# An already tuned three-stage fp32 kernel on one core: the second MLP's input product done as Strassen's seven half-size products, with streamed weights and one written instruction list

## The chip, the core and the metric

The kernel runs on one NeuronCore of a Trainium2 chip. Its engines run side by side, each through its own instruction list and in that list's order: TensorE (PE) multiplies matrices, VectorE (DVE), ScalarE (ACT) and GpSimd (POOL) work elementwise, and SyncE (SP) issues the transfers between DRAM and the on-chip memory SBUF. TensorE writes only to PSUM, eight banks of 128 partitions by 512 fp32 columns; ACT and DVE read the results from there. The metric is the device time of one execution in microseconds (us); lower is better.

## The reference

Three stages follow each other on 2304 tokens (T): a decayed linear attention of 4 batches, 8 heads, 576 positions; a first MLP (512 to 1024 to 512 with softmax, gating and layer norm); a second MLP (512 to 2048 to 512):

```python
h = x @ w_in                     # x: 2304 x 512, w_in: 512 x 2048
g = np.where(h >= 1, h, np.where(h <= -1, 0.0, (h + 1) ** 2 / 4.0))
return (g @ w_out).astype(np.float32)
```

Every matmul is in fp32 accuracy: an operand is split into a rounded part (hi) and the rest (lo), and a product is three TensorE matmuls, hi*lo, lo*hi and hi*hi, summed in PSUM. The weights arrive as 64-bit words and are first turned into fp32 on the chip.

## The kernel before

**Stages and their lists.** The attention, the first MLP and the preparation of all weights stand in ORDER, a table of words that one loop plays: each word (such as `H.3.0.4`) is a step and appends that step's instructions to the engines' lists. Attention steps are `q`, `k` (loads of a 128-token tile), `S`, `I`, `O`, `U` (matmuls) and others; the first MLP has `H` (hidden product, 12 matmuls 512 columns wide), `T` (transposes) and `J` (output product, 48 matmuls 256 wide, of 256 tokens each); `G`, `B` and `t` take its result to DRAM (`xsd`). `l` to `g` turn one unit of weights into hi and lo, `h` makes the sums that Strassen's scheme wants of the second MLP's output weights (on POOL), `s` stores the prepared weights to DRAM (`wid` input weights, `wod` output weights).

**The second MLP** is written out in code behind ORDER. The tokens are cut in blocks of 512 (four, and one last block of 256); the 2048 hidden units in 8 pairs of 128-unit chunks. A *slot* is one block with one pair: 32 slots of 512 tokens, 8 of 256. For each slot `hidden(s, i)` makes chunk i of the pair: 12 matmuls 512 tokens wide (line 565: four 128-row slices of the inner dimension times three matmuls) into the one PSUM bank `h2`. ACT reads it twice (`r`, line 573; `h`, line 574), DVE makes the activation `g` (lines 575 and 580). `factors(s)` makes the seven left factors of Strassen's scheme for the *output* product (line 588) and splits them into `gh` and `gl` (lines 135, 136). `project(s, part)` is that output product: seven half-size products for each 256 tokens, 3 matmuls 256 wide each (line 613), so 42 matmuls for a slot of 512 tokens; they accumulate in the other seven banks over the 8 pairs of a block, and `project_end` adds the sums up (line 643). TensorE's list takes hidden and project in turn, the projection two slots behind:

```python
for s in range(2, len(slots) + 2):
    for i in range(2):
        if s < len(slots):
            hidden(s, i, ps2, "h2")
            ...
        project(s - 2, i)
```

All 16 chunks of the input weights are loaded once and stay in SBUF (`wi`, 512 KB each). The output weights (1792 KB for a pair, as seven half-size matrices, hi and lo) are streamed: three are in SBUF, and `load_wo` fetches the next when one comes free. The blocks go through the pairs alternately forward and backward, so three pairs are met again without a load. PE's and SP's orders in this stage are as the code is written; the other engines' orders are chosen by the framework's scheduler. At the switch from `ps` to `ps2` the second MLP's PSUM banks take the place of the first MLP's.

Of the kernel before, what the change touches and what calls it, by code (L numbers as in the profile page):

```python
# [11 lines left out]
F32 = mybir.dt.float32  # L12
# [10 lines left out]
T = B * S  # L23
DM = H * D
# [16 lines left out]
b.1 O.2 c.1 f.7 V.3 U.2 P.3 H.0.0.4 k.4 W.2 d.1 b.13 D.2 e.8 X.2 g.7 e.1 l.15 a.13.3 f.8 Y.2 c.13 S.4.6.0 f.1
R.0.0 I.3.5 b.9 d.13 g.8 U.3 q.5 a.9.2 V.4 e.13 O.3 W.3 c.9 l.10 b.15 g.1 U.4 k.6 f.13 P.4 I.4.3 d.9 W.4 D.3 O.4
q.6 a.15.0 g.13 X.3 e.9 S.5.6.5 k.5 b.10 c.15 l.12 Y.3 H.0.1.2 f.9 P.5 V.6 a.10.5 D.4 c.10 d.15 X.4 H.1.1.6
R.0.1 d.10 e.15 l.17 f.15 m.0 e.10 V.5 I.5.3 E.0.0 R.1.1 l.19 g.9 E.0.1 U.5 q.8 M.0.0 O.5 f.10 g.15 M.0.1 W.5
z.0 S.6.0.4 k.8 a.12.2 g.10 Y.4 Q.0.0 x.0 I.6.5 P.6 Q.0.1 U.6 q.7 b.12 m.1 w.0 S.8.0.4 E.1.0 c.12 r.0 O.6 D.5
W.6 V.8 N.0.0 M.1.0 H.2.0.3 k.7 E.1.1 d.12 P.8 N.0.1 x.1 X.5 M.1.1 a.17 Y.5 T.0.0.1 z.1 e.12 b.17 I.7.0 Q.1.1
R.2.0 l.20 V.7 H.3.0.4 D.6 K.0.0 c.17 Q.1.0 L.0.0 d.17 f.12 w.1 X.6 g.12 U.7 r.1 a.19 R.3.0 H.3.1.6 Y.6 N.1.1
W.7 e.17 N.1.0 c.19 l.18 a.20 T.1.1.5 b.19 R.3.1 I.8.1 K.1.1 m.3 c.20 b.20 d.19 L.1.1 T.0.1.2 q.9 O.8 K.0.1
L.0.1 b.18 d.20 H.2.1.5 k.9 D.8 e.20 X.8 l.16 Y.8 T.1.0.2 R.2.1 Z.0 f.17 H.4.1.1 V.9 K.1.0 E.3.0 L.1.0 m.2 E.3.1
M.3.0 E.2.0 g.17 J.0.0.2 x.3 E.2.1 s.17 M.2.0 f.20 x.2 a.18 M.2.1 b.16 z.2 M.3.1 Q.2.1 z.3 c.18 Q.2.0 g.20 Q.3.1  # L50
d.18 w.2 S.9.4.3 s.20 G.0.0 U.9 q.13 P.9 r.2 Q.3.0 H.4.0.5 W.9 B.0.0 N.2.0 w.3 t.0.0 N.2.1 e.18 a.16 e.19 l.28
T.2.0.6 R.4.0 r.3 l.24 O.9.3 R.4.1 h.19.0 N.3.0 S.7.4.2 k.11 D.9 h.19.1 N.3.1 J.0.1.3 q.10 P.7 h.19.2 X.9 f.19.0
Y.9 b.28 m.4 g.19.0 a.24 a.28 c.16 b.24 c.28 c.24 V.11 S.10.2.4 K.2.0 G.0.1 L.2.0 d.16 O.7 B.0.1 H.5.0.6 P.10
k.10 h.19.3 t.0.1 d.28 f.19.1 D.7 X.7 e.16 T.3.1.3 g.19.1 l.23 f.16 T.3.0.2 K.3.1 T.2.1.4 R.5.0 V.10 s.19 I.10.0
E.4.0 L.3.1 Y.7 E.4.1 U.10 q.11 M.4.0 K.3.0 O.10 M.4.1 d.24 W.10 z.4 K.2.1 H.5.1.3 k.12 x.4 L.3.0 Q.4.0 L.2.1
Q.4.1 D.10 b.23 w.4 U.11 X.10 R.5.1 r.4 J.1.0.5 W.11 m.5 g.16 N.4.0 e.28 s.16 E.5.0 e.24 l.22 E.5.1 M.5.0 Y.10
l.29 N.4.1 M.5.1 V.12 f.28 z.5 x.5 Q.5.1 g.28 Q.5.0 U.12 s.28 T.4.0.1 G.1.0 w.5 I.11.2 a.23 r.5 B.1.0 f.24 c.23
S.11.4.0 t.1.0 W.12 d.23 N.5.1 I.13.6 q.12 P.11 N.5.0 J.1.1.3 a.22 g.24 b.29 c.22 s.24 b.22 a.29 d.22 c.29 e.22
e.23 l.31 T.5.1.5 K.4.0 d.29 l.30 T.4.1.0 G.1.1 L.4.0 I.12.4 K.5.1 B.1.1 h.23.0 K.4.1 H.8.0.1 L.5.1 t.1.1 h.23.1
L.4.1 b.31 h.23.2 a.31 e.29 f.23.0 H.6.0.3 R.8.0 h.23.3 l.26 b.30 c.31 g.23.0 f.29 a.30 g.29 f.23.1 T.5.0.5  # L60
# [55 lines left out]
def net(ctx: ExitStack, tc: tile.TileContext, qk_t, kv, w_in1, w_out1, g_ln, w_in2, w_out2, masks, decay, out):  # L116
# [198 lines left out]
    def e(u):  # L315
# [232 lines left out]
    def load_wo(s, spare=False):  # L548
# [3 lines left out]
        if p in wo:  # L552
            return
# [216 lines left out]
```

## Time and profile before

| | us |
|---|---|
| median of 3 runs (703.21 to 704.28) | 703.65 |
| the profiled execution's own time | 704.7 |
| its span, first to last instruction | 702.9 |
| TensorE busy in the span | 673.8 |
| VectorE busy | 483.6 |
| ScalarE busy | 364.6 |
| GpSimd busy | 161.8 |

The profiled execution took 1.8 us more than its span, and is 1.05 us above the median of the runs. "Busy" counts an instruction from its start to its end; TensorE's matmuls overlap in the pipeline, so that a busy TensorE can still do more or less work in the same time. Its rate is read from the distance between starts.

### The profile page before, as it was taken

The page shows a single profiled execution, that of the slowest core. Times are in us where ns is not written, and L with a number is a line of the kernel's source. Part 1 is how long each engine was busy: PE and PEld are TensorE (multiplying, and loading weights), DVE is VectorE, ACT ScalarE, POOL GpSimd, SP SyncE. Part 2 cuts the span into 40 slices and gives each one's busy share as a digit, 9 for nine tenths or more (in the row PEclk, how much of TensorE's full clock was granted, in tenths as well). Part 3 has the DMA queues.
Part 4 walks back from the last instruction along what each step waited for, and adds up shares of the span by engine and source line. Part 5 has one row for each costly group of instructions (what it writes and reads, how often), then busy time and mean ns, then how long its engine had stood idle before and what let it go on. Part 6 is the DMA issues. An engine that isn't in the chain of part 4 may idle for free.

```text
span 702.9 us, 12647 instructions
## 1 busy us (share of the span) xinstructions
PE 673.8 (96%) x5000; PEld 603.4 (86%) x5000; DVE 483.6 (69%) x926; ACT 364.6 (52%) x666; POOL 161.8 (23%) x166
## 2 busy tenths in 40 slices
PE   4699999999999999997999999999999999999996
PEld 3587888888988989886998998898898898899996
DVE  4778687878768887544656676657756567556875
ACT  4769768667847678732423433434433343333442
POOL 4987455556365652000000000000000000000000
PEclk9699999999999999999999999999999999999999
DMA  9975569697897897994445315452245403345292
GB/s 334 402 249 208 179 202 368 227 350 267 261 290 269 317 343 295 392 388 154 155 159 210 120 61 210 142 187 106 92 178 210 165 31 133 131 187 210 79 340 91
DMA packets 35547, 152.76 MB, mean 217 GB/s; under 512 B 3616, under 2 KB 11936, under 8 KB 30240
## 3 DMA queue, kind: packets, MB, share of 16 engines
q1 hardware_dynamic: 35200, 151.54, 59.2%
q8 instruction: 39, 0.64, 0.4%
q10 hardware_dynamic: 288, 0.42, 0.2%
q14 instruction: 20, 0.16, 0.1%
HBM read 114.72 MB, written 37.22 MB: 216 GB/s over the span
## 4 chain that ended last, share of the span: by engine, by line
PE 90%; DMA 7%; issue 1%; DVE 1%; ACT 0%; POOL 0%; SPq 0%; DVEq 0%; POOLq 0%; ACTq 0%
PE h L565 29%; PE bank L400 14%; PE bank L502 13%; PE pa L613 7%; PE pb L613 7%; PE pc L613 7%; PE pd L613 4%; DMA qk<-in_qk_t 4%; PE bank L195 2%; PE bank L225 2%; PE bank L472 2%; PE bank L213 2%; DMA kv<-in_kv 2%; DMA st<-in_w_out 2%; PE bank L236 1%
## 5 line engine op out<-in xcount | busy, mean ns | idle before, releaser
L565 PE MATMUL h<-xs,wi 128*128 128x512 f32 (+1 forms) x960 | 215.7, 374 | 3.9 <-issue 3.9
L565 PEld LDWEIGHTS h<-xs,wi 128*128 128x128 f32 x960 | 164.8, 189 | 33.1 <-issue 4.1
L573 ACT ACTIVATE r<-h 128x512 f32<-128x512 f32 (+1 forms) x80 | 44.4, 555 | 163.2 <-PE h L565 163.0
L575 DVE SCALAR_TENSOR_TENSOR r<-r 128x512 f32<-128x512 f32 (+1 forms) x80 | 50.9, 636 | 112.6 <-ACT r L573 112.6
L135 ACT ACTIVATE gh<-gs 128x1024 fp32r<-128x1024 f32 (+1 forms) x80 | 66.9, 873 | 77.5 <-DVE gs L588 73.3
L502 PE MATMUL bank<-ln,wo 128*128 128x256 f32 x864 | 102.1, 278 | 0.0
L502 PEld LDWEIGHTS bank<-ln,wo 128*128 128x128 f32 x864 | 100.4, 188 | 1.2
L400 PE MATMUL bank<-wi1h,x 128*128 128x512 f32 x288 | 90.6, 396 | 0.0
L136 DVE TENSOR_TENSOR gl<-gs,gh 128x1024 fp32r<-128x1024 f32 (+1 forms) x80 | 77.1, 996 | 13.5 <-ACT gh L135 13.5
L310 POOL TENSOR_TENSOR y<-y,st 128x512 int32<-128x512 int32 x48 | 66.6, 1390 | 53.9 <-DVE y L306 27.6
L613 PE MATMUL pb<-wo,gh 128*128 128x256 f32 x288 | 75.2, 283 | 0.0
L400 PEld LDWEIGHTS bank<-wi1h,x 128*128 128x128 f32 x288 | 54.7, 190 | 11.6
L613 PE MATMUL pc<-wo,gh 128*128 128x256 f32 x288 | 63.5, 283 | 0.0
L613 PE MATMUL pa<-wo,gh 128*128 128x256 f32 x288 | 63.0, 281 | 0.0
L588 DVE TENSOR_TENSOR gs<-gs 128x256 f32<-128x256 f32 (+1 forms) x160 | 60.1, 396 | 3.6
L400 PE MATMUL bank<-wi1l,x 128*128 128x512 f32 x144 | 59.7, 415 | 0.0
L580 DVE TENSOR_TENSOR gs<-h,r 128x512 f32<-128x512 f32 (+1 forms) x80 | 51.0, 638 | 7.7 <-DVE r L575 0.9
L613 PEld LDWEIGHTS pb<-wo,gh 128*128 128x128 f32 x288 | 55.0, 191 | 0.0
L613 PEld LDWEIGHTS pa<-wo,gh 128*128 128x128 f32 x288 | 49.5, 190 | 2.6
L613 PEld LDWEIGHTS pc<-wo,gh 128*128 128x128 f32 x288 | 50.0, 192 | 0.0
L574 ACT COPY h<-h 128x512 f32<-128x512 f32 (+1 forms) x80 | 43.1, 539 | 0.0
L613 PE MATMUL pa<-wo,gl 128*128 128x256 f32 x144 | 40.7, 283 | 0.2 <-DVE gl L136 0.2
(82 smaller groups left out, 1080.8 us busy)
## 6 DMA issues: line engine op xcount, KB each, us to landing
wo<-wod SPq DMA_DIRECT2D x28, 1792.0 KB, 7.3
wod<-wo SPq DMA_DIRECT2D x8, 1792.0 KB, 7.3
st<-in_w_in SPq DMA_DIRECT2D x24, 512.0 KB, 6.7
st<-in_w_out SPq DMA_DIRECT2D x24, 512.0 KB, 5.2
qk<-in_qk_t SPq DMA_DIRECT2D x18, 512.0 KB, 5.5
kv<-in_kv SPq DMA_DIRECT2D x18, 512.0 KB, 5.7
xsd<-x SPq DMA_DIRECT2D x36, 256.0 KB, 5.2
wid<-wi SPq DMA_DIRECT2D x16, 512.0 KB, 4.3
```

The costliest lines, as they stand in the source:

```text
L135: nc.scalar.activation(hi, src, AF.Copy)
L136: eng.tensor_tensor(out=lo, in0=src, in1=hi.bitcast(F32), op=ALU.subtract)
L310: nc.gpsimd.tensor_tensor(out=yd[u].bitcast(I32), in0=yd[u].bitcast(I32), in1=raw_w[u][:, :, 0].bitcast(I32), op=ALU.add)
L400: nc.tensor.matmul(hp, a[:, kk, :], w[:, fs], start=(n == 0), stop=(n == 3 * KD - 1))
L502: nc.tensor.matmul(px[:, mm, :], w[:, ms], a[:, f, :], start=(n == 0), stop=(n == 3 * C1 - 1))
L565: nc.tensor.matmul(hp[:, :n], wi[c][:, w, kk], xs[b][:, a, kk], start=(k == 0), stop=(k == 3 * KD - 1))
L573: nc.scalar.activation(r[:, :n], hp[:, :n], AF.Relu, bias=0.5, scale=0.5)
L574: nc.scalar.copy(h[:, :n], hp[:, :n])
L575: nc.vector.scalar_tensor_tensor(out=r[:, :n], in0=r[:, :n], scalar=1.0, in1=r[:, :n], op0=ALU.min, op1=ALU.mult)
L580: nc.vector.tensor_tensor(out=g, in0=h_, in1=r_, op=ALU.max)
L588: nc.vector.tensor_tensor(out=g[:, o], in0=g[:, x], in1=g[:, y], op=op)
L613: nc.tensor.matmul(po[key][:, half], a[:, x, t], wo[p][0][:, w, y], start=(begin and j == 0), stop=(last and j == 2), skip_group_check=True,)
```

## The change

The input product of the second MLP is rewritten for the 32 slots of 512 tokens. The 512 tokens are cut in halves, the 512 inner rows in halves and the pair's 256 hidden units in halves, and Strassen's scheme makes the product from seven products of half size: each is 2 inner slices times 3 matmuls, 256 tokens wide, so 42 matmuls of 256 columns take the place of 24 of 512. The last 256 tokens (`tp`) are multiplied as before, 24 matmuls of 256 columns for a pair.

What goes with it:
- The input weights of a pair become seven half-size matrices, hi and lo, 1792 KB in place of 1024; `h` makes their sums on POOL for both MLP weights. They no longer fit, so they are streamed like the output weights, three pairs in SBUF (`wi`: 23 loads in all; output weights: 27, four of them `wt`).
- The x of a block is loaded raw (`xr`), its four sums are made (`xc`) and its seven factors are split (`xh` on ACT, `xl` on DVE; for block 0 partly on POOL). `B` and the stores of x's lo are gone.
- The seven products of a slot go through *one* PSUM bank in four groups (`hp.s.0` 12 matmuls, `hp.s.1` 6, `hp.s.2` 12, `hp.s.3` 12). After each group ACT copies the bank out (`ha`) before the next group may write. DVE puts the pieces together (`hA`, `hB`); then follow `hr` and `hq` (Relu and Square on ACT), `hm` and `hg` (min and max on DVE), the factors `hf`, and the split `hh`, `hl`.
- The output product (`pp`) is cut in five chunks of 9, 12, 7, 7 and 7 matmuls that stand between the groups. Its last of the seven products is now the one for bank `d`.
- The last 256 tokens' activations go through DRAM once (`ts`, `tL`) and have their output product (`tj`) at the very end, after the last `pp`.
- ORDER runs to the end of the kernel, and sets the order on all engines; the part for the first two stages is a new order too. No bank is set up anew at the switch.

```diff
-C.6 l.6 q.0 k.0 q.1 l.2 l.5 l.0 l.3 k.1 a.6.0 l.11 C.1 b.6 c.6 l.4 S.0.1.2 l.14 d.6 l.8 C.5 C.0 V.0 e.6 C.3 q.2
+C.6 q.0 C.0 k.0 l.1 k.1 q.1 l.3 l.2 l.6 S.0.0.1 l.0 l.7 C.2 l.10 C.5 V.0 P.0 q.2 C.3 l.11 U.0 l.8 a.1.2 C.1 b.1
...
+ha.11.3 wi.14 hf.10.2 hf.10.3 hh.10.0 hA.11 hp.12.0 hh.10.1 hl.10.0 hr.11.0 pp.9.1 hl.10.1 ha.12.0 hB.11 hp.12.1
...
-        y = ws[units[u][1] // 2]
-        o, x, z = ((4, 1, 0), (1, 3, 1), (5, 3, 4), (6, 2, 5))[n]
-        nc.gpsimd.tensor_tensor(out=y[:, o], in0=y[:, x], in1=y[:, z], op=ALU.subtract)
+        y = ws[u]
+        if units[u][0] == 2:
+            o, x, z, op = ((4, 2, 3, ALU.add), (2, 0, 2, ALU.subtract), (5, 4, 0, ALU.subtract), (6, 1, 5, ALU.subtract))[n]
+        else:
+            o, x, z = ((4, 1, 0), (1, 3, 1), (5, 3, 4), (6, 2, 5))[n]
+            op = ALU.subtract
+        nc.gpsimd.tensor_tensor(out=y[:, o], in0=y[:, x], in1=y[:, z], op=op)
...
-        c, n = 2 * p + i, blocks[b][1]
-        hp = pool.tile([P, BLK], F32, tag=tag, name="h2")
-        k = 0
-        for kk in range(KD):
-            for w, a in ((1, 0), (0, 1), (0, 0)):
-                nc.tensor.matmul(
-                    hp[:, :n], wi[c][:, w, kk], xs[b][:, a, kk], start=(k == 0), stop=(k == 3 * KD - 1)
-                )
-                k += 1
+    GROUPS = (((0, 0), (1, 1)), ((2, 1),), ((3, 0), (4, 1)), ((5, 1), (6, 0)))
+    def hp_(s, n, place=7):
+        b, p = slots[s]
+        if n == 0:
+            hp[s] = bank(place, [P, 2, 2 * P])
+        w = resident["wi"][p][0]
+        for o, half in GROUPS[n]:
+            x = xs[b, o][0]
+            k = 0
+            for kk in range(2):
+                for u, a in ((1, 0), (0, 1), (0, 0)):
+                    nc.tensor.matmul(
+                        hp[s][:, half], w[:, u, SLOT[o], kk * P : (kk + 1) * P], x[:, a, kk],
+                        start=(n in (0, 3) and half == 0 and k == 0), stop=(k == 5), skip_group_check=True,
+                    )
+                    k += 1
+            if s % 8 == 7:
+                ring.append(xs.pop((b, o))[1])
+    def ha(s, n):
+        if n == 0:
+            sn[s] = act1.tile([P, 3, 2 * P], F32, tag=f"x1{s % 2}", name="sn")
+        if n == 2:
+            hc[s] = act1.tile([P, 2, 2, 2 * P], F32, tag=f"e{s % 2}", name="hc")
+        if n == 1:
+            nc.scalar.copy(sn[s][:, 0], hp[s][:, 1])
+        else:
+            nc.scalar.copy(sn[s][:, 1:3] if n == 0 else hc[s][:, (1, 0)[n - 2]], hp[s])
+    def hA(s):
+        nc.vector.tensor_tensor(out=hc[s][:, 1], in0=hc[s][:, 1], in1=sn[s][:, 0:2], op=ALU.add)
+    def hB(s):
+        nc.vector.tensor_tensor(out=hc[s][:, 0, 0], in0=hc[s][:, 0, 0], in1=sn.pop(s)[:, 2], op=ALU.add)
+    def hr_(s, k):
+        hr[s, k] = stage.tile([P, 2, 2 * P], F32, tag="y", name="r", bufs=3)
+        nc.scalar.activation(hr[s, k], hc[s][:, 1 - k], AF.Relu, bias=0.5, scale=0.5)
+    def hm(s, k):
+        nc.vector.tensor_scalar(hr[s, k], hr[s, k], 1.0, None, op0=ALU.min)
+    def hq(s, k):
+        nc.scalar.activation(hr[s, k], hr[s, k], AF.Square)
+    def load_for(kind, s):
+        full = len(resident[kind]) == 3
+        if kind == "wo" and s == len(slots) - 1:
+            home = resident["wi"].pop(slots[s - 2][1])[1]
+        else:
+            home = resident[kind].pop(slots[s - 3][1])[1] if full else homes[kind, s]
+        load14(kind, slots[s][1], home)
+    CHUNKS = (0, 9, 21, 28, 35, 42)
+    def pp(s, c):
+        b, p = slots[s]
+        w = resident["wo"][p][0]
+        for i in range(CHUNKS[c], CHUNKS[c + 1]):
+            product(b, i, s % 8 == 0, s % 8 == 7, ghl[s], w)
```

**TensorE's list in the middle of the second MLP, before.** `h` is the hidden bank, `xs` the tokens, `wi` the input weights; `pa`, `pb`, `pd` are banks of the output product; "waits" names the engine whose work the row needs first, DMAHW is a transfer.

```order
L565 MATMUL h_4359<-xs,wi_3710 128x512 [waits Activation_49]
L565 MATMUL h_4359<-xs,wi_3710 128x512 x11
L613 MATMUL pa<-wo_4171,gh 128x256 [waits DMAHW6_49]
L613 MATMUL pa<-wo_4171,gl 128x256 [waits DVE_49]
L613 MATMUL pa<-wo_4171,gh 128x256 x2
L613 MATMUL pa<-wo_4171,gl 128x256
L613 MATMUL pa<-wo_4171,gh 128x256
L613 MATMUL pb<-wo_4171,gh 128x256
L613 MATMUL pb<-wo_4171,gl 128x256
L613 MATMUL pb<-wo_4171,gh 128x256
```

The same place in the changed kernel (the groups `hp` are line 712 with the bank as `bank<-xs,wi`, the chunks `pp` line 799):

```order
L712 MATMUL bank<-xs,wi 128x256 [waits Activation_49]
L712 MATMUL bank<-xs,wi 128x256 x5
L799 MATMUL bank<-wo,gl 128x256
L799 MATMUL bank<-wo,gh 128x256 x2
L799 MATMUL bank<-wo,gl 128x256
L799 MATMUL bank<-wo,gh 128x256 x2
L799 MATMUL bank<-wo,gl 128x256
L712 MATMUL bank<-xs,wi 128x256 [waits Activation_49]
L712 MATMUL bank<-xs,wi 128x256 x11
L799 MATMUL bank<-wo,gh 128x256 x2
```

A wait on ACT stood every 33 matmuls, behind 21 of the projection; now one stands in front of each group of 12 or 6, here behind 7.

**ScalarE's list in the same stage, one slot, before.**

```order
L573 ACTIVATE r<-h_5221 128x512 [waits PE_49]
L574 COPY h<-h_5221 128x512 [waits Activation_49]
L573 ACTIVATE r<-h_5262 128x512 [waits PE_49]
L574 COPY h<-h_5262 128x512 [waits DVE_49]
L135 ACTIVATE gh<-gs 128x1024 [waits DVE_49,PE_49]
L135 ACTIVATE gh<-gs 128x768 [waits DVE_49]
```

In the changed kernel about a slot's work (lines 727 and 729 are the copies `ha`, 743 `hr`, 751 `hq`, 777 `hh`):

```order
L777 ACTIVATE gh<-gs 128x1024 [waits DVE_49]
L743 ACTIVATE r<-hc 128x512 [waits DVE_49]
L729 COPY hc<-bank 128x512 [waits PE_49]
L729 COPY sn<-bank 128x512 [waits PE_49]
L751 ACTIVATE r<-r 128x512 [waits DVE_49]
L743 ACTIVATE r<-hc 128x512 [waits DVE_49]
L727 COPY sn<-bank 128x256 [waits PE_49]
L777 ACTIVATE gh<-gs 128x768 [waits DVE_49]
L751 ACTIVATE r<-r 128x512 [waits DVE_49]
```

Six instructions of a slot became ten, and the copies that TensorE waits for now stand between others that wait for DVE.

**SyncE's transfer list in the second MLP, before** (`wo<-wod` is a load of output weights, `out<-osb` a store of results):

```order
L556 DMA wo_4940<-wod_123 128x3584 [waits PE_49]
L556 DMA wo_5033<-wod_122 128x3584 [waits DMAHW6_49,DMAHW1_49,PE_49]
L556 DMA wo_5126<-wod_121 128x3584 [waits DMAHW7_49,DMAHW2_49,PE_49]
L540 DMA xs<-xsd_132 128x4096 [waits DMAHW3_49,PE_49]
L645 DMA out<-osb 128x512 [waits DMAHW4_49,DVE_49,Activation_49]
```

And in the changed kernel at the same block (`wi<-wid` a load of input weights, `xr` of raw x):

```order
L632 DMA wi<-wid_111 128x3584 [waits DMAHW7_49,DMAHW0_49,PE_49]
L632 DMA wo<-wod_116 128x3584 [waits PE_49]
L632 DMA wi<-wid_112 128x3584 [waits DMAHW1_49,PE_49]
L667 DMA xr<-xsd_124 128x1024 [waits DMAHW2_49]
L667 DMA xr<-xsd_124 128x1024 [waits DMAHW3_49]
L632 DMA wo<-wod_117 128x3584 [waits DMAHW4_49,PE_49]
```

The loads of output weights now alternate with loads of input weights of the same size, each issued when TensorE is done with the pair whose place it takes.

## Rows read from the trace of the kernel before

**Rows 1.** The page's first line.

```profile
span 702.9 us, 12647 instructions
```

**Rows 2.** Stretches: length; PE, PEld, DVE, ACT, POOL busy; PE clock, DMA share, GB/s.

```profile
0.00:30.00 30.00, 13.86 (x145) 12.10 (x145) 17.70 (x30) 19.19 (x33) 18.84 (x21) 0.81 0.96 363
...
60.00:285.00 225.00, 223.72 (x1848) 195.62 (x1845) 176.20 (x360) 162.68 (x318) 116.51 (x119) 1.00 0.78 275
286.00:297.60 11.60, 10.65 (x95) 10.41 (x94) 5.64 (x20) 9.05 (x19) 1.49 (x4) 1.00 0.99 420
...
324.70:644.40 319.70, 319.70 (x1981) 287.07 (x1982) 200.88 (x337) 119.61 (x184) 0.00 (x0) 0.99 0.41 151
```

**Rows 3.** The chain that ended last, in order of time: start, length, what.

```profile
29.99 4.01 PE bank L400 x12
...
34.00 1.09 PE bank L195 x16
...
285.02 10.92 PE bank L502 x96
...
320.80 3.88 issue
324.69 4.57 PE h L565 x12
...
331.78 2.79 PE h L565 x12
...
639.16 2.80 PE h L565 x12
```

**Rows 4.** Timeline of ACT and DVE at the switch to the second MLP.

```profile
322.17 0.58 ACT L514 ACTIVATE x<-bank 128x512 fp32r<-128x512 f32 x1
...
319.88 4.10 DVE L136 TENSOR_TENSOR gl<-gs,gh 128x1024 fp32r<-128x1024 f32 x4 [0.70 <-ACT gh L135]
323.90 0.69 DVE L519 TENSOR_TENSOR x<-bank,x 128x512 fp32r<-128x512 f32 x1
```

**Rows 5.** Timeline: one hand-over from PE to ACT, one from ACT to PE.

```profile
408.54 0.28 PE L613 MATMUL pa<-wo,gh 128*128 128x256 f32 x1
...
408.74 0.60 ACT L573 ACTIVATE r<-h 128x512 f32<-128x512 f32 x1 [3.69 <-PE h L565]
...
296.46 0.80 ACT L464 ACTIVATE e<-e,sm 128x512 f32<-128x512 f32 x1
...
297.32 0.66 PE L472 MATMUL bank<-ident,e 128*128 128x128 f32 x4 [0.95 <-ACT e L464]
```

**Rows 6.** Groups by line and shape on DVE, ACT and POOL: busy us, mean ns.

```profile
L588 DVE TENSOR_TENSOR gs<-gs 128x256 f32<-128x256 f32 x128 | 51.5, 423 | 2.9
L580 DVE TENSOR_TENSOR gs<-h,r 128x512 f32<-128x512 f32 x64 | 44.3, 692 | 6.3 <-DVE r L575 0.5
...
L136 DVE TENSOR_TENSOR gl<-gs,gh 128x1024 fp32r<-128x1024 f32 x32 | 39.2, 1225 | 11.3 <-ACT gh L135 11.3
L136 DVE TENSOR_TENSOR gl<-gs,gh 128x768 fp32r<-128x768 f32 x32 | 30.5, 952 | 0.0
...
L306 DVE TENSOR_SCALAR y<-y 128x512 uint32<-128x512 uint32 x32 | 17.0, 539 | 3.5 <-ACT y L297 3.5
...
L573 ACT ACTIVATE r<-h 128x512 f32<-128x512 f32 x64 | 38.4, 599 | 147.5 <-PE h L565 147.5
...
L135 ACT ACTIVATE gh<-gs 128x1024 fp32r<-128x1024 f32 x32 | 33.9, 1061 | 65.2 <-DVE gs L588 62.8 <-PE bank L502 2.4
...
L135 ACT ACTIVATE gh<-gs 128x768 fp32r<-128x768 f32 x32 | 26.7, 833 | 0.0
...
L377 POOL TENSOR_TENSOR ws<-ws 128x256 f32<-128x256 f32 x32 | 26.0, 822 | 4.7 <-DVE ws L325 2.9 <-ACT e L423 0.9
```

**Rows 7.** DVE near the end: the split of a half-width slot, both parts.

```profile
694.31 1.16 DVE L136 TENSOR_TENSOR gl<-gs,gh 128x512 fp32r<-128x512 f32 x2 [0.23 <-ACT gh L135]
```

**Rows 8.** DMA issues: what, queue, count, KB each, median us to landing.

```profile
wo<-wod SPq DMA_DIRECT2D x28, 1792.0 KB, 7.3
```

More of the change, by code (lines that the diff above doesn't have):

```diff
@@ L41 @@
[L41 to L60, printed above, removed]
@@ new lines, in net, with product @@
+    BANK = {("a", 0): 0, ("b", 0): 1, ("d", 0): 2, ("c", 0): 3, ("a", 1): 4, ("b", 1): 5, ("c", 1): 6}
+    CHUNKS = (0, 9, 21, 28, 35, 42)
+    def product(b, i, first, last, g, w, tail=False):
+        t, (x, y, name, half) = i // 21, PRODUCTS[i // 3 % 7]
+        j = i % 3
+        if name == "d":
+            half, key = t, (b, "d", 0)
+        else:
+            key = b, name, t
+        if key not in po:
+            po[key] = bank({"a": 7, "d": 0, "b": 1, "c": 3}[name] if tail else BANK[key[1:]], [P, 2, 2 * P])
+        begin = first and j == 0 and half == {"a": 0, "b": 1, "c": 1, "d": 0}[name]
+        a, u = ((0, 1), (1, 0), (0, 0))[j]
+        nc.tensor.matmul(
+            po[key][:, half], g[a][:, x, t], w[:, u, y], start=begin, stop=(last and j == 2), skip_group_check=True
+        )
@@ L644, in project_end, with tx @@
-        for i in range(2):
-            (nc.scalar if i and b == len(blocks) - 1 else nc.sync).dma_start(rows[:, i], o[:, i])
-    gs = {}
-    @step
-    def i(c):
-        load_wi(c, w2a, f"w{c}")
+        (nc.scalar if i and b == NB else nc.sync).dma_start(rows[:, i], osb[b, t][:, i])
+    tailx, tgt, tgs = {}, {}, {}
+    @step
+    def tx(_):
+        tailx["raw"] = stage.tile([P, 2, 2, 2 * P], F32, tag="st", name="tx")
+        nc.sync.dma_start(tailx["raw"].rearrange("p h k t -> p (h k) t"), xsd[NB])
@@ new lines, in tr, with tc_, tm, tq @@
+    @step
+    def tr(k):
+        tgt[k] = stage.tile([P, 2, 2, 2 * P], F32, tag="st", name="tr")
+        nc.scalar.activation(tgt[k][:, 0], hp["t"], AF.Relu, bias=0.5, scale=0.5)
+    @step
+    def tc_(k):
+        nc.scalar.copy(tgt[k][:, 1], hp["t"])
+    @step
+    def tm(k):
+        nc.vector.tensor_scalar(tgt[k][:, 0], tgt[k][:, 0], 1.0, None, op0=ALU.min)
+    @step
+    def tq(k):
+        nc.scalar.activation(tgt[k][:, 0], tgt[k][:, 0], AF.Square)
+    @step
+    def tg(k):
+        x = tgt[k]
+        nc.vector.tensor_tensor(out=x[:, 1], in0=x[:, 1], in1=x[:, 0], op=ALU.max)
```

569 lines of the change are left out of this document (356 added, 213 removed).

## The prediction

> **What bounds the kernel now.** I read the stretches first. In the second MLP (324.7 to 644.4) TensorE is busy in all of its 319.7 us, DVE in 200.88 (63%), ACT in 119.61 (37%), and the transfers run at 151 GB/s [rows 2]. From 60 to 285 us, attention and first MLP, TensorE is busy in 223.72 of 225. Only the first 30 us are loose: 13.86 us busy, at a mean clock of 0.81, while the transfers run at 363 GB/s. Then the chain in order of time: from 331.78 to 639.16 it is a series of half slots, 12 matmuls 512 wide in 2.79 us and then the projection's 21 of 256 [rows 3]. There are 58 half slots in 307.38 us, 5.30 us each with no gap between them. So the kernel is a sum of TensorE's matmuls. What is saved there is saved in the end, as long as nobody makes TensorE wait.
>
> The two rates follow. 12 of 512 columns take 2.79 us, 0.2325 us each; the remaining 2.51 us are 21 of 256 columns, 0.1195 each. Half the columns cost 51.4% of the time, not 50%: about 0.0065 us a matmul does not depend on the width.
>
> One wait stands out: 3.88 us at 320.80, and the 12 matmuls behind it take 4.57 us, not 2.79, at half clock [rows 3]. It ends with the work on the first MLP's last output, whose bank `h2` takes over: ACT copies it at 322.17 and DVE finishes at 323.90 + 0.69 = 324.59, because four splits (4.10 us from 319.88) stand ahead of it on DVE [rows 4].
>
> **The change, part by part.**
>
> *Fewer columns.* 32 slots had 24 matmuls of 512: 768 x 0.2325 = 178.6 us. They get 42 of 256: 1344 x 0.1195 = 160.6 us. **-18.0 us.** The number of output products and the last 256 tokens' matmuls stay as they are. The rate is taken from the projection, since there, as in the new groups, the accumulator changes every few matmuls. The best rate of 256 columns is that of the first MLP's output product, 96 in 10.92 us [rows 3], 0.1138 each: that would be 153 us, -25.7.
>
> *A rule that speaks against it.* The row: the projection loads new weights for every 256 columns and keeps 0.1195 us, so a load that is not hidden costs at most the 0.0065 above, 576 x 0.0065 = 3.7 us for the extra matmuls, which the 160.6 holds. The Trainium skill, TensorE: Matmul & The Clock Gate, Part 3 (The mechanism), says that weight loads overlap running matmuls only when their row groups differ; here all use all rows. By it, with the page's 128 columns at 1.2 GHz for a load, a pair would be an estimated 0.21 us, and the change would lose some 108 us. The trace here does not agree with that.
>
> *The wait at the switch goes.* No bank is handed over behind DVE's splits, so 3.88 + (4.57 - 2.79) = **-5.7 us**.
>
> *Rounds through one bank.* Each group waits for ACT's copy of the group before. ACT starts 0.20 us after TensorE has begun its next work (408.54, 408.74), copies 512 columns in 0.60, and TensorE goes on 0.06 after ACT's end (296.46 + 0.80, 297.32) [rows 5]: 0.86 us. In the changed order of matmuls I counted what stands between two groups: in 57 of the rounds 7 matmuls (0.84 us), in most others 9 to 21 (1.08 to 2.51 us). With ACT free on time the 57 lose 0.02 us each. With a 0.60 us instruction ahead each time they lose 0.60 x 57 = 34 us. ACT's load per slot by [rows 6]: four copies, four Relu/Square at most 0.60 each, and 1.06 + 0.83: 6.7 us, with the x splits (7 x 0.60 per 8 slots) 7.2 of 10.04 us. A slot worked through by hand (slot 12's last group to slot 14's first) had all four copies done before their chunk ended, the closest by 0.1 us. So I take the low end: 57 x 0.05 = **+3 us** (0 to 34).
>
> *DVE.* Per slot by [rows 6]: `hA` 0.69, `hB` 0.42, two `hm` 0.54 (line 306 is the nearest scalar operation), two `hg` 0.69, four `hf` 0.42, `hl` 1.23 + 0.95: 7.4 us. Per block there come `xc` and `xl`, 11 x 0.69 = 7.6, and 14 sums of results at 0.42 = 5.9, or 1.7 a slot. Together 9.1 of a slot of 84 x 0.1195 = 10.04 us, 91%. The same sum for before is 7.4 of 10.6, 69%, where the window shows 63%; so some 83% in a window. It fits, but at a block's end six `xl` fall in one slot: 7.4 + 4.1 = 11.5 against 10.04, 1.5 us behind. What covers it: from a slot's last group to its projection stand 110 matmuls, 13.1 us, and the chain between (copy 0.86, `hB`, Relu, min, Square, max, factors 1.7, two splits) adds up to 7.7. If the cover goes, the projection waits for `hl` first. Three block ends at 1 us: **+3 us** (0 to 9).
>
> *The new switch.* The first two input-weight loads wait for the last hidden product of the first MLP, since they take its weights' place: 3.67 MB, at the 420 GB/s of 286 to 297.6 [rows 2] 8.7 us. Over them lie two output products, 10.92 us, and a transpose. The second-last output product then waits for the last transposes' hi and lo. **+2 us** (0 to 6, the old wait's size).
>
> *The tail.* The last eight projections, 21 x 0.1195 = 2.51 us each, follow one another; before, hidden products stood between them. DVE needs for each four narrow factors, a split of 1.16 [rows 7] and one sum of 0.42. The narrow split is 53% of the wide one's 2.18; at that share the factors are 0.9, in all 2.5, level with TensorE; at full width 3.3. **+1 us** (0 to 6).
>
> *Attention and first MLP.* Their matmuls are the same. DVE loses `B` (18 x 0.69 = 12.4 us); POOL gains 32 sums at 0.82, 26.3 us, beside the 116.51 of 225 us that it is busy now [rows 2, 6], so there is room; if it were full, stores of weights would be late, which are first read at the switch. The new order moves two tiles' attention (eight groups of about 1 us, as 1.09 at 34.00) ahead of the first hidden product, which before started at 29.99 [rows 3], into time in which TensorE waits for loads. But the last weights needed there now stand behind more loads; I expect that product at about 36. 7.7 us of work moved, 6 us later: **-2 us**, between -8 and +5, as it comes at 30 or 43.
>
> *Streaming* is costed at nothing. In five of eight slots both kinds of weights are loaded, 3.67 MB in 10.04 us, 366 GB/s. A load alone lands in 7.3 us [rows 8] and is issued two slots, 20 us, ahead. Behind such a load in SP's list stand result stores and raw x, none needed within a slot.
>
> Sum: -18.0 - 5.7 + 3 + 3 + 2 + 1 - 2 = -16.7. From the span of 702.9 [rows 1] that is 686.2. The profiled execution took 1.8 us more than its span; the median is 0.75 above the span, so **687 us** on the scale of the runs.
>
> **The rivals.**
> *The best rate.* The groups run at the first MLP's 0.1138: 687 - 7.7 = 679. For it: six matmuls in a row share an accumulator; against: the old hidden matmuls shared one over 12, and were no nearer to their best.
> *Rounds paced by ACT.* ACT's list now mixes TensorE's copies with steps that wait for DVE; a copy behind one that is late waits too. At 0.3 us in each of the 57 tight rounds: +17 in place of +3, 701.
> *DVE becomes the bound, slower than before.* Eight of its twelve instructions in a slot start on an ACT result. At 0.2 us idle for each, a slot is 9.1 + 1.6 = 10.7 us against 10.04: 32 x 0.66 = 21 us, 708. It decides from 0.52 us a slot (16.7 / 32), a slot of 10.56. For it: 91% by sum; against: in the old slots DVE's starts are mostly waits for TensorE, and instructions overlap.
> *Transfers too slow.* The lead of 20 us is eaten when five slots' loads take over 14.04 us each, below 262 GB/s. At 230 they lose about 9.6 us in each of four blocks: 725. Against: 420 GB/s when asked [rows 2].
>
> **How the numbers follow.** Forecast 0.62 (by itself 679 to 694), best rate 0.12, rounds 0.13, DVE 0.10, transfers 0.03. By what a measurement of this kernel can tell, 0.2% is 1.4 us: faster is below 702.2. Forecast and best rate fall there, of the rounds two thirds, of DVE a fifth: 0.62 + 0.12 + 0.09 + 0.02 = 0.85; 0.03 for no change; slower 0.12. The range goes from the best rate with 4 us more gained at the start, 675, to the paced rounds, 701.
>
> **What would show it.** In the new profile: a slot of 84 matmuls every 10.0 to 10.4 us; ACT's copies starting 0.2 us after a group, and few waits of line 712 on ACT over 0.3 us; DVE's busy share of 80 to 88% there; no wait near 4 us at the switch; line 712's waits for a load at zero. I am wrong if slots take over 10.5 us, and the engine that the waits of lines 712 and 799 name says why; or if the last hidden product of the first MLP ends more than 8 us from 285.02, where the output product behind it starts [rows 3].

## The result and the profile after

The changed kernel takes **683.85 us** (median of 4 runs, 682.14 to 686.16), the kernel before 703.96 beside it (703.21 to 704.88): ratio 0.9716, 95% interval 0.9684 to 0.9747. Run again it took 684.04, ratio 0.9726 (0.9714 to 0.9739). Each experiment was timed with the kernel before beside it and is read against that ratio: a difference of two kernels is the difference of their ratios times 703 us, and their intervals leave it open by 1 to 3 us. Forecast were 687 us. The profiled execution took 686.16 us, its span is 684.4, to be held against 702.9 [rows 1].

The page's first lines:

```profile
span 684.4 us, 14038 instructions
...
PE 658.0 (96%) x5576; PEld 618.6 (90%) x5576; DVE 520.5 (76%) x996; ACT 453.6 (66%) x817; POOL 206.2 (30%) x206
```

The stretches, with the columns of [rows 2]. The last output product of the first MLP begins at 286.2, the switch ends at 327.85, 549.10 is 22 slots on, and the tail begins at 649.35.

```profile
0.00:30.00 30.00, 13.29 (x146) 11.09 (x148) 16.51 (x28) 16.83 (x29) 17.91 (x21) 0.80 0.96 365
60.00:285.00 225.00, 223.31 (x1888) 195.44 (x1889) 178.25 (x348) 166.10 (x316) 149.91 (x153) 1.00 0.71 259
...
297.30:327.85 30.55, 30.19 (x259) 29.95 (x257) 15.00 (x25) 18.72 (x35) 2.73 (x4) 1.00 1.00 397
327.85:549.10 221.25, 220.04 (x1830) 217.66 (x1828) 180.81 (x328) 144.90 (x246) 0.00 (x0) 1.00 0.70 267
...
649.35:684.40 35.05, 29.61 (x243) 29.01 (x242) 26.10 (x72) 11.73 (x22) 0.00 (x0) 0.99 0.66 249
```

Twenty-two slots in 221.25 us are 10.06 us each, in place of 10.6, with TensorE busy in 99.5% of them. DVE is at 82%, as forecast for a window. At the switch, where TensorE stood still for 3.88 us [rows 3], it is busy in 30.19 of 30.55. In the tail it works from 649.35 to its last matmul's end at 679.29 with one stop of 0.33; the rest is the last sums and stores, as before. From 60 to 285 us POOL took on the added sums (149.91 us where there were 116.51).

All that TensorE waits for in the second MLP, by what ended the wait (us in total, times, longest):

```profile
PE bank L712 <- ACT sn L727: 0.8, 2, 0.5
PE bank L799 <- DVE osb L823: 0.7, 1, 0.7
PE bank L799 <- DVE gl L932: 0.3, 1, 0.3
```

No load is among them. The chain in order of time (start, length, what), where [rows 3] had 285.02:

```profile
286.22 10.90 PE bank L593 x96
...
652.32 7.60 DMA gtd<-tr
659.98 3.91 DMA tg<-gtd
666.19 11.32 PE bank L799 x89
```

So the last output product of the first MLP begins 1.2 us later than before, and from there to the end the kernel takes 398.2 us in place of 417.9: 19.7 less.

What this view of waits leaves out shows in a timeline of TensorE and ACT (start, duration, engine, line, count, and in brackets the idle time ahead):

```profile
503.15 1.57 PE L712 MATMUL bank<-xs,wi 128*128 128x256 f32 x12
504.56 0.28 PE L799 MATMUL bank<-wo,gh 128*128 128x256 f32 x1
...
504.76 0.59 ACT L729 COPY hc<-bank 128x512 f32<-128x512 f32 x1 [1.00 <-PE bank L712]
...
505.15 0.40 PE L799 MATMUL bank<-wo,gh 128*128 128x256 f32 x2
505.41 1.68 PE L712 MATMUL bank<-xs,wi 128*128 128x256 f32 x12
506.92 0.28 PE L799 MATMUL bank<-wo,gl 128*128 128x256 f32 x1
```

The group at 503.15 had 9 matmuls of the projection ahead of it and hands over after 1.41 us (504.56). The one at 505.41 had 7, and hands over after 1.51 us, though it has the same twelve matmuls. The hand-over is as it was forecast: ACT begins 0.20 us after TensorE's next work (504.76), copies in 0.59, and TensorE goes on 0.06 later: 0.85 us after 504.56. TensorE waits for it some 0.01 us, too little for the waits above, and yet it loses 0.1. The same two places in narrow windows, matmuls and weight loads that begin there:

```profile
503.04 0.66 PEld L712 LDWEIGHTS bank<-xs,wi 128*128 128x128 f32 x5
...
503.15 0.63 PE L712 MATMUL bank<-xs,wi 128*128 128x256 f32 x4
...
505.40 0.53 PEld L712 LDWEIGHTS bank<-xs,wi 128*128 128x128 f32 x4
505.41 0.62 PE L712 MATMUL bank<-xs,wi 128*128 128x256 f32 x3
```

Without a wait the weights are loaded 0.11 us ahead of their matmul (503.04, 503.15), under the one before, and four matmuls fit into 0.63 us. After a wait the load begins with the matmul (505.40, 505.41), and three take as long: the load is not hidden. In the records such a matmul lasts 0.386 us and the next begins 0.225 after it, where the others last 0.279 and follow at 0.118: **0.107 us for such a wait, even one of 0.01 us.** From the first hidden group on 55 matmuls last over 0.363 us (bare loads, below), 47 of them of line 712. Of the 55 groups with 7 matmuls ahead of them 40 are among these, of those with 12 and more none. The Trainium skill, TensorE: Matmul & The Clock Gate, Part 2 (LDWEIGHTS), gives 128 columns at 1.2 GHz for a load, an estimated 0.107 us. The trace agrees, but only where TensorE had to wait; behind a running matmul the load is hidden here (0.118 us from start to start), so that this is no return of the rule that spoke against the change.

### The profile page after: what moved, and what is told of

Same layout as the page of the kernel before. It is cut to its first block, busy times and chain, and to the rows that moved or that the text cites. A ratio compares the mean times of both kernels' runs of the same rounds, so it can differ in the third digit from the quotient of the medians.

```text
span 684.4 us, 14038 instructions
## 1 busy us (share of the span) xinstructions
PE 658.0 (96%) x5576; PEld 618.6 (90%) x5576; DVE 520.5 (76%) x996; ACT 453.6 (66%) x817; POOL 206.2 (30%) x206
## 4 chain that ended last, share of the span: by engine, by line
PE 80%; DMA 7%; DVE 6%; ACT 2%; POOL 2%; issue 1%; SPq 0%; DVEq 0%; POOLq 0%
PE bank L712 23%; PE bank L799 23%; PE bank L491 12%; PE bank L593 11%; PE bank L868 3%; PE bank L288 2%; PE bank L318 2%; PE bank L563 2%; DVE ws L460 2%; DMA qk<-in_qk_t 1%; PE bank L306 1%; DMA gtd<-tr 1%; PE bank L329 1%; DMA st<-in_w_in 1%; DMA kv<-in_kv 1%
## 5 line engine op out<-in xcount | busy, mean ns | idle before, releaser
L799 PE MATMUL bank<-wo,gh 128*128 128x256 f32 x1008 | 194.0, 281 | 0.7 <-DVE osb L823 0.7
L712 PE MATMUL bank<-xs,wi 128*128 128x256 f32 x1344 | 183.4, 284 | 0.8 <-ACT sn L727 0.8
L712 PEld LDWEIGHTS bank<-xs,wi 128*128 128x128 f32 x1344 | 166.6, 188 | 3.9 <-ACT sn L727 1.3
L799 PEld LDWEIGHTS bank<-wo,gh 128*128 128x128 f32 x1008 | 160.6, 189 | 1.0 <-DVE osb L823 1.0
L799 PE MATMUL bank<-wo,gl 128*128 128x256 f32 x504 | 142.2, 282 | 0.3 <-DVE gl L932 0.3
L491 PE MATMUL bank<-wi,x 128*128 128x512 f32 x432 | 107.7, 400 | 2.6 <-DVE xf L345 1.1
L491 PEld LDWEIGHTS bank<-wi,x 128*128 128x128 f32 x432 | 78.8, 188 | 21.8 <-DVE e L519 1.4
L799 PEld LDWEIGHTS bank<-wo,gl 128*128 128x128 f32 x504 | 95.4, 189 | 0.7 <-DVE gl L932 0.5
L777 ACT ACTIVATE gh<-gs 128x1024 fp32r<-128x1024 f32 x64 | 59.8, 951 | 8.0 <-DVE gs L767 4.3
L472 POOL TENSOR_TENSOR ws<-ws 128x256 f32<-128x256 f32 x64 | 55.4, 877 | 8.5 <-DVE ws L418 6.7
```

What stands on the lines that cost most here:

```text
L472: nc.gpsimd.tensor_tensor(out=y[:, o], in0=y[:, x], in1=y[:, z], op=op)
L491: nc.tensor.matmul(hp, a[:, kk, :], w[:, fs], start=(n == 0), stop=(n == 3 * KD - 1))
L712: nc.tensor.matmul(hp[s][:, half], w[:, u, SLOT[o], kk * P : (kk + 1) * P], x[:, a, kk], start=(n in (0, 3) and half == 0 and k == 0), sto ...
L777: nc.scalar.activation(ghl[s][0][:, i], gs[s][:, i], AF.Copy)
L799: nc.tensor.matmul(po[key][:, half], g[a][:, x, t], w[:, u, y], start=begin, stop=(last and j == 2), skip_group_check=True)
```

## The experiments

**1. Even chunks, and tight ones.** A projection is issued in five chunks, and hidden groups stand between them. The diff is that of even; tight has 0, 9, 27, 32, 37, 42.

```
-    CHUNKS = (0, 9, 21, 28, 35, 42)
+    CHUNKS = (0, 9, 18, 26, 34, 42)
```

> The five chunks of a projection are cut at 9, 18, 26, 34 in place of 9, 21, 28, 35, so that the 55 rounds with 7 matmuls between two groups have 8 (0.96 us by 0.1195, not 0.84). Theory, the hand-over of a bank takes 0.86 us, as predicted: 55 x 0.02 = 1.1 us gained. By the trace after, where a group of six behind 7 matmuls takes 0.81 to 0.83 us and not 0.70, a tight round loses 0.11 and the gain is 55 x 0.11 = 6 us at most. Rival, the groups are slow for another reason (ACT late, the accumulator): no change, or a loss where a chunk now begins ahead of its factors.

> Cuts at 9, 27, 32, 37: the 55 rounds have 5 matmuls (0.60 us) in place of 7. Theory, TensorE waits for what is left of the hand-over and nothing else: 0.86 - 0.60 = 0.26 us in each, against 0.02, so +13 us; if the hand-over is 0.95, as 0.11 lost behind 7 would have it, 0.35 against 0.11, the same +13. Rival, ACT's copy is late by more once rounds follow each other so closely: 0.60 more where one instruction stands ahead, over +20. Rival, other rounds of the same slot give the time back: under +5.

Even: 679.12 us, ratio 0.9662 (0.9646 to 0.9678), 4.5 us less than the changed kernel. In it a chunk ends within the sum that ACT copies at a block's end, so that ACT copies it one matmul early. Tight: 695.25 us, 0.9884 (0.9868 to 0.9900), 11.1 us more, with 13 expected. The timeline of tight:

```profile
500.17 1.68 PE L712 MATMUL bank<-xs,wi 128*128 128x256 f32 x12
...
501.88 0.59 ACT L729 COPY hc<-bank 128x512 f32<-128x512 f32 x1 [1.24 <-PE bank L712]
...
502.52 1.68 PE L712 MATMUL bank<-xs,wi 128*128 128x256 f32 x12
```

A round is 2.35 us: group 1.51, then 0.20, 0.59 and 0.05 of the hand-over, though only 5 matmuls stand in between. In its records 71 matmuls have the bare load, all 55 groups behind 5 among them, and the waits ahead of them sum up to 13.7 us, where the changed kernel has 55 and 3.2: +10.5 and +1.7. The rivals of a late ACT and of time given back fall. Even missed its theory of 1.1 us, which counts the wait alone, and stays under its bound of 6; what the wait brings with it is put to the test next.

**2. Even chunks with whole sums.** The cuts of even, and in ORDER three words move: `pc.0.1`, `pc.1.1` and `pc.2.1` (ACT's copy for the second half) stand behind `pp.7.3`, `pp.15.3` and `pp.23.3`, one chunk later.

> The cuts at 9, 18, 26, 34 once more, with ACT's copy at a block's end (second half) moved behind the chunk that now completes its sum, in three blocks, so that all sums are complete. Theory: by the traces a tight round costs not its 0.01 to 0.02 us of waiting alone but 0.107 more, since the weight load of the group's first matmul waits too and is then not hidden (its matmul lasts 0.386 and not 0.279 us). With 8 matmuls between groups some 32 of these 48 go: 32 x 0.12 = 3.8 us, and 0.7 at a block's start, as in the kernel cut so before: 679 to 680. Rival: the gain came from sums read too early and goes with them: 684.

680.9 us, ratio 0.9676 (0.9656 to 0.9696): 3.5 us less than the changed kernel, the fastest whole version of this study. The two intervals leave that between 1.8 and 5.2; the rival had nothing gained. 25 bare loads are left of 55 in the repeated run, and of the 55 groups that now have 8 matmuls ahead 3 show one; 30 x 0.12 = 3.6. The rounds in its timeline, all as the undisturbed one above:

```profile
498.07 1.57 PE L712 MATMUL bank<-xs,wi 128*128 128x256 f32 x12
...
500.43 1.59 PE L712 MATMUL bank<-xs,wi 128*128 128x256 f32 x12
...
502.81 1.57 PE L712 MATMUL bank<-xs,wi 128*128 128x256 f32 x12
```

**3. The accumulator.** Halves take turns:

```
-        for o, half in GROUPS[n]:
-            for kk in range(2):
-                for u, a in ((1, 0), (0, 1), (0, 0)):
+        for k in range(6):
+            kk, (u, a) = k // 3, ((1, 0), (0, 1), (0, 0))[k % 3]
+            for o, half in GROUPS[n]:
```

> In the hidden groups of 12 matmuls, which fill first one half of a bank with six and then the other, the two halves take turns after every matmul: 12 changes of accumulator in place of 2. Same matmuls, weights and columns. The trace after gives 0.1135 us a matmul where 24 share an accumulator, 0.1175 where six do and 0.1195 where three do: a change of accumulator would cost about 0.02 us. Theory, that is the cause of the rates between 0.1138 and 0.1195: 3 groups x 10 changes x 0.02 x 32 slots = +19 us. Rival, the rate hangs on something else (the width and the operands): no change within 2 us.

682.65 us, ratio 0.9719 (0.9703 to 0.9735): no change. (This kernel leaves a part out: in the last group of a slot the bank is begun anew when one matmul of the other half is already in it, and that half's sum so far drops out.) The theory falls: a change of accumulator costs nothing. Hidden matmuls follow each other at 0.1178 us on the mean in both traces, while the output product of line 593 has 0.114 to 0.115. What sets the difference stays open.

**4. More matmuls.** The first six of a slot are issued twice:

```
-        for o, half in GROUPS[n]:
+        for again, (o, half) in enumerate(GROUPS[n][:1] * (n == 0) + GROUPS[n]):
```

> Six more matmuls of 256 columns in each of the 32 slots: the first group's six are issued twice, and the second time begins the bank anew, so that what is computed stays. Theory, the end is the sum of TensorE's matmuls: 192 x 0.1175 to 0.1195 = +22.6 to +22.9 us on 684.0. Rival, something else sets the pace of a slot and TensorE has room: less than half of it. A second rival, from the prediction: DVE is the bound or next to it; then a longer slot gives DVE room and the added matmuls cost clearly less than 22 us.

704.30 us, ratio 1.0018 (1.0007 to 1.0028): 20.5 us more of the 22.6. TensorE's work sets the time; about a tenth of what is added to it found room.

**5. More work on DVE, and less.** The upper half is dve3, on the changed kernel; the lower half even2pool, on even2.

```
-        nc.vector.tensor_tensor(out=g[:, o], in0=g[:, x], in1=g[:, y], op=op)
+        for _ in range(4 if n == 0 else 1):
+            nc.vector.tensor_tensor(out=g[:, o], in0=g[:, x], in1=g[:, y], op=op)
...
-        nc.vector.tensor_scalar(hr[s, k], hr[s, k], 1.0, None, op0=ALU.min)
+        nc.gpsimd.tensor_scalar(hr[s, k], hr[s, k], 1.0, None, op0=ALU.min)
```

> DVE computes the first factor of each slot four times in place of once (the same numbers): 3 x 0.42 = 1.26 us more in each of 32 slots. DVE was busy in 82% of a slot of 10.06 us after the change, 8.2 us, so it comes to 9.5, 94%. Theory, TensorE is the bound and DVE has 1.8 us left in a slot: only the block ends, where six splits of x fall in one slot, come later; +0 to +5 us. Rival, DVE's idle time is made of waits for ACT that it can't use: most of 32 x 1.26 = 40 us is added, over +15.

> The same, and line 747, two instructions of 0.42 us in each slot, runs on POOL, which is idle in the second MLP, and not on DVE. 1.26 us more a slot on DVE cost 0.54 us a slot, so DVE has some 0.7 us to spare. Theory: without added work DVE makes TensorE wait hardly at all, and 0.85 us less on it gives nothing, within 2 us of the kernel cut the same way. Rival: DVE is next to the bound already and some us are gained, 3 or more. Rival on the other side: POOL takes about twice DVE's time (0.82 against 0.42 for 256 columns), which lengthens the chain from a group to its factors by 0.9 us a slot: slower by 3 or more.

dve3: 701.23 us, ratio 0.9971 (0.9955 to 0.9987), 17.2 us more, 0.54 a slot of the 1.26 added. So the rival, and the theory falls. But DVE isn't full: from 350 to 550 us it is busy in 173.42 of 200, 87%, when TensorE loses 8.2 us there. What ends TensorE's waits is ACT in all but one, from 297 us on:

```profile
PE bank L712 <- ACT sn L727: 2.9, 5, 1.1
PE bank L712 <- ACT hc L729: 2.9, 6, 0.8
PE bank L712 <- ACT sn L729: 2.7, 6, 1.0
PE bank L800 <- DVE osb L824: 2.1, 1, 2.1
PE bank L869 <- ACT hc L729: 0.8, 1, 0.8
```

In all 18 waits on ACT its copy starts without a gap behind another instruction of its list, and in 15 of them one of the three instructions ahead had waited for DVE. The loss isn't even: by the starts of the slots, against the repeated run, 15 of 31 slots lose 0.3 us or less, and seven lose 1.26 to 2.49, four of them in a row behind the first block's end. So 0.54 is a mean, and the room differs from slot to slot.

even2pool says it from the other side. DVE has 0.85 us less in a slot, and the kernel takes 701.39 us, 0.9968 (0.9956 to 0.9979), 20.5 more than even2. POOL takes 1.53 us (median) for line 747, DVE 0.42, so the way from a group to its factors grows by 2.2 us a slot. The place where it hurts, in its timeline:

```profile
443.37 3.48 POOL L747 TENSOR_SCALAR r<-r 128x512 f32<-128x512 f32 x2 [7.96 <-ACT r L743]
...
445.03 0.87 PE L712 MATMUL bank<-xs,wi 128*128 128x256 f32 x6
...
446.87 0.63 ACT L751 ACTIVATE r<-r 128x512 f32<-128x512 f32 x1 [1.19 <-POOL r L747]
...
447.41 0.35 ACT L727 COPY sn<-bank 128x256 f32<-128x256 f32 x1
...
447.82 1.69 PE L712 MATMUL bank<-xs,wi 128*128 128x256 f32 x12 [0.97 <-ACT sn L727]
```

The group of six at 445.03 is done before 446. ACT could copy it, but its list has the Square of line 751 first, which waits for POOL until 446.87. The copy comes at 447.41, and TensorE stands for 0.97 us. That is the rival "rounds paced by ACT" of the prediction, called up by a longer chain. 4.9 us more are four waits for ACT's reading of the last 256 tokens' bank (`tr`, `tc`), which stands behind such Squares too. The unchanged list stands close to it: of 1.26 us more in the chain it covers 0.72 on the mean. Whether 0.85 us less on DVE would gain anything by itself this run doesn't show, since the chain grew with it.

**6. More transfers.** The diff is that of loads; loads2 copies `wid[p][:, 0]`, half of it.

```
     def load14(kind, p, home):
+        if kind == "wi":
+            spare[len(spare)] = y = dram.tile([P, 2, 7, 2 * P], F32, name=f"spare{len(spare)}")
+            nc.sync.dma_start(y, wid[p])
```

> Beside each load of input weights 1.83 MB more are moved, from the same array to an unused one in device memory, 32 times: 59 MB. In five of eight slots that makes 5.5 MB in 10.06 us, 547 GB/s, over the 420 that were seen. Theory, weights are asked for two slots ahead (20 us), so a block's five slots fall behind by 5 x (13.1 - 10.06) = 15 us by the 420 and the lead still covers it: within 3 us of no change. Rival, the transfers have no room: from the second of the five slots on TensorE waits for a load, 15 us in each of four blocks, +30 to +60.

> The kernel as changed, with half of the extra transfers: 0.92 MB beside each load of input weights, 29 MB in all. The full 59 MB cost 48.7 us. Theory: the transfers of the second MLP (272 GB/s over its 398 us, 108 MB) come to 137 MB, 344 us at 400 GB/s, under the 398 that TensorE takes, so the reserve covers nearly all of it: 0 to +8, most of it at the switch, where the transfers already run at 391 GB/s. Rival: what is hurt is each burst of loads, and half the bytes cost half the time: +24.

The copies were counted too high ahead of the runs, with 32, 59 and 29 MB. Input weights are loaded 23 times, and both traces have 23 copies (transfers issued: count, KB each, us to landing; loads, then loads2). That makes 42 MB and 21 MB.

```profile
spare<-wid SPq DMA_DIRECT2D x23, 1792.0 KB, 14.9
...
spare<-wid SPq DMA_DIRECT2D x23, 896.0 KB, 10.5
```

loads: 732.67 us, ratio 1.0421 (1.0381 to 1.0461), 48.9 more; loads2: 694.9 us, 0.9879 (0.9858 to 0.9900), 10.8 more. For the full amount the theory falls, and the rival has the size but not the place. The stage as a whole has room for 108 + 42 MB, 375 us at 400 GB/s. But by the starts of the slots, against the repeated run, 30.6 us are lost in the first eight slots, each of which loads both kinds of weights; in loads2 these have 10.5 of its 11.5 us. There the transfers have no room (a stretch of loads, columns of [rows 2]):

```profile
327.00:349.00 22.00, 20.79 (x177) 20.56 (x177) 14.86 (x27) 13.99 (x25) 0.00 (x0) 1.00 1.02 418
```

TensorE's waits for loads in loads2 are four, with the longest at the switch (timeline, bracketed part):

```profile
301.48 2.05 PE L717 MATMUL bank<-xs,wi 128*128 128x256 f32 x12 [3.95 <-DMA wi<-wid]
...
314.88 3.08 PE L717 MATMUL bank<-xs,wi 128*128 128x256 f32 x24 [0.83 <-DMA wi<-wid]
...
364.01 1.67 PE L717 MATMUL bank<-xs,wi 128*128 128x256 f32 x12 [0.16 <-DMA wi<-wid]
...
377.22 2.55 PE L717 MATMUL bank<-xs,wi 128*128 128x256 f32 x12 [2.06 <-DMA wi<-wid]
```

7.0 of the 10.8 us are these. In the later blocks the lead of two slots does cover the weights, nearly. What loads loses there, 5.6 and 8.4 us in one slot each of the second and third block, comes by another way (its timeline):

```profile
472.73 0.69 DVE L687 TENSOR_TENSOR xt<-xr 128x512 f32<-128x512 f32 x1 [6.14 <-DMA xr<-xsd]
473.46 0.63 ACT L692 ACTIVATE xs<-xt 128x512 fp32r<-128x512 f32 x1 [5.24 <-DVE xt L687]
...
475.65 0.57 ACT L734 COPY sn<-bank 128x512 f32<-128x512 f32 x1
...
476.27 1.65 PE L717 MATMUL bank<-xs,wi 128*128 128x256 f32 x6 [3.79 <-ACT sn L734]
```

The next block's raw x lands late (17.1 us after its issue, 10.1 in the changed kernel). DVE's sum waits for it, ACT's split for that, and ACT's copy of the bank stands behind the split: TensorE waits 3.79 us, and 6.39 at the same place one block on, for a transfer whose data it doesn't need yet. Streaming is hidden in the changed kernel, but the switch has no reserve at all and the slots after it little.

**7. The old switch without its wait.** The kernel before, with one more name in a list that fixes the order of the banks:

```
-    for key in (0, "a", 0), (0, "b", 0), (0, "d"), (0, "c", 0), (0, "a", 1), (0, "b", 1):
+    for key in (0, "a", 0), (0, "b", 0), (0, "d"), (0, "c", 0), (0, "a", 1), (0, "b", 1), (0, "c", 1):
```

> The kernel before with one change: its output bank for the last of eight sums is assigned ahead of the hidden products' bank, so that the hidden product at the switch takes over another bank than the one that DVE still reads behind its splits. Theory, the wait of 3.88 us and the half clock behind it go and are not given back: 5.7 us less than before. Rival, half of it comes back because the projection behind it then waits for the factors: 2 to 3 us less. Rival, the wait was for something else: no change.

697.15 us, ratio 0.9919 (0.9900 to 0.9938), 5.7 us less than before (4.4 to 7.0). The half clock of the kernel before stands in this stretch, behind the wait (columns of [rows 2]):

```profile
327.00:329.00 2.00, 2.00 (x6) 1.59 (x5) 0.00 (x0) 0.00 (x0) 0.00 (x0) 0.50 0.91 262
```

The timeline without the wait, where [rows 3] had 320.80, 324.69 and 4.57:

```profile
317.90 2.96 PE L565 MATMUL h<-xs,wi 128*128 128x512 f32 x12
320.70 0.28 PE L613 MATMUL pa<-wo,gh 128*128 128x256 f32 x1
```

The hidden product follows the output product at once, and the projection follows it at full clock (1.00 granted from 300 to 324 us). The whole term is there, and nothing comes back. So 5.7 of the change's 20 us were to be had without it.

**8. The first load.** On even2, one word moves in ORDER: `S.0.0.1 q.2 l.0 l.7 C.2 l.10 C.5 V.0 P.0` in place of `S.0.0.1 l.0 l.7 C.2 l.10 C.5 V.0 P.0 q.2`.

> The same cuts, and the third tile's load of q and k is issued four weight loads earlier, right behind the first tile's scores. TensorE waits 6.4 us for it at 22.95. Theory: loads land in the order of issue at some 1.3 us for 512 KB, so it lands 5 us earlier, but the next tiles' loads come no sooner and TensorE waits for those: 0 to 3 us gained. Rival: all 5 us are gained. Rival: the weights behind it are late instead and the first hidden product comes later: slower by up to 2.

682.11 us, ratio 0.9696 (0.9676 to 0.9716): no gain over even2's 0.9676, within the intervals. The load's wait falls to 1.8 us from 5.5 in even2 (6.4 in the changed kernel), and others take its place:

```profile
PE bank L288 <- DMA qk<-in_qk_t: 5.7, 2, 5.0
PE bank L288 <- DVE wi L460: 4.2, 2, 3.8
PE bank L318 <- POOL kv L278: 2.9, 1, 2.9
PE bank L306 <- DMA qk<-in_qk_t: 1.8, 1, 1.8
```

## Why the prediction was right, step by step

The forecast was 686.2 for a span that came out at 684.4. The steps:

*Fewer columns*, -18.0. Mis-sized. Hidden matmuls follow each other at 0.1178 us, not at the projection's 0.1195: 1344 x 0.1178 = 158.3, **-20.3**. The projection, too, runs at 0.1183 where it had 0.1194 (means of undisturbed distances in both traces): 1512 x 0.0011 = -1.7 that no step had. Neither comes to the 0.114 of the best rate, and with experiment 3 the reason that was given for either rate, how often the accumulator changes, is gone.

*The rule against it.* No sign of 108 us; what there is of unhidden loads is 55 x 0.107 = 5.9 us, behind waits alone.

*The old wait*, -5.7: **5.7 by experiment 7**.

*Rounds through one bank*, +3. The hand-over of 0.86 us was right (0.85), and 55 groups have 7 matmuls ahead where 57 were counted. The price was too low: 47 groups cost 0.12 us each, 5.6 in all (even2 gives back 3.5 of it), because a wait of 0.01 us brings 0.107 for the bare load. The predicted 0.05 for a group had no such part.

*DVE at block ends*, +3: one wait of 0.74 at the first block's end, with its load **0.85**; the other two block ends cost nothing. At the second block's beginning one group follows another with nothing in between, 0.7 more, which no step had. "DVE becomes the bound" was put too narrowly as a rival. Experiment 5 shows that a slot has 0.7 us of room on the mean, some have none, and not the 1.8 of DVE's idle time, and that the engine that then stops TensorE is ACT, whose list is in order. The 13.1 us of cover against 7.7 of chain, by which I had 5.4 us of room, left that out.

*The new switch*, +2: 0.36 us of idle time and a few bare loads, under 1. *The tail*, +1: 0.3, at the chain's link through the last stores and loads (652.32 to 663.89).

*Attention and first MLP*, -2. Here the step failed: work moved into waits was to be free, with the hidden product 6 us later. That product begins at 39.0 us, not at 36. Over eleven profiled executions with the new order it begins 33.4 us after the first matmul (32.4 to 34.1), in two with the old order 23.7, so 9.7 us later for 7.7 us of moved work. The moved groups were to fill waits for loads, but TensorE is busy in 13.29 us of the first 30 where it was in 13.86: it waits for the loads of q and k of those very tiles (6.4 and 5.2 us) and for POOL's product behind one of v (3.0). The last output product begins 279.1 us after the first matmul (mean of the eleven, 277.9 to 280.9) against 278.8 and 276.0, 1.7 later. The first matmul itself comes 1.0 us earlier (5.1 against 6.1), so from the span's start it is **+0.6** on the mean (282.8 to 286.1 against 284.9 and 282.1), and +1.2 in the profile above. Two executions of the old order don't tell this from zero, but the gain of 2 isn't seen. Experiment 8 shows that this one load alone is not to blame.

*Streaming*, 0: right, no wait for a load, though landing takes 8.6 us and not 7.3. The rival looked for the danger in the weights' lead over five slots of each block. Experiment 6 shows it in the first eight slots, and in the raw x, which the forecast held not to be needed within a slot: when it is late, ACT's list carries that to TensorE.

For the second MLP these sum up to -20.3 - 1.7 - 5.7 and, for all waits from the first hidden group on with their loads, 3.2 + 5.9: -18.6 of the measured -19.7. 1.1 us is not assigned.

That the sum came within 2 us is in part luck. The columns gave 4.0 us more than forecast, and the first stages 3.2 less. The four terms for waits, +9 together, met 9.1, but most of that is bare loads, which none of them held.

## What to carry to other kernels

Where weights change with every matmul, count the waits and not only their length: even one of 10 ns can show a weight load that is otherwise hidden, so a matmul more between two uses of a bank can be worth a tenth of a microsecond each time. An engine's idle share says little of its reserve when its list is in order and it also frees the bound engine's banks: lengthen the chain by a known amount and see how much of it comes through. A transfer's lead protects that transfer alone: look also at what lands behind it in the same queue, and at whose list waits for it. Work moved into a wait fills it only if its own data are there earlier than what the wait was for.

## What was not expected of the hardware

- A matmul that had to wait shows its weight load: 0.386 us and 0.225 to the next, against 0.279 and 0.118 (55 of them, 5.9 us).
- A change of accumulator after every matmul costs nothing (0.1178 us a matmul either way).
- POOL needs 1.53 us (median) for a minimum with a constant on 128x512, and 1.49 when no DVE instruction runs beside it (eight of 64); DVE needs 0.42. The Trainium skill, GPSIMD Engine Reference, 4.1 (Engine selection), has one-input operations at roughly line rate there; this run does not agree.
- 21 MB of extra copies within device memory cost 10.8 us, and twice that 48.9, 30.6 of them in the first eight slots: it is the bursts that are full, not the stage.
